# A MoE kernel with attention beside it: the late attention writes x transposed and normalises it by products with ones

## The chip, the core and the metric

The kernel runs on one NeuronCore of a Trainium2 chip. The metric is the device time of one execution in microseconds; the median of several runs is compared. The engines are TensorE (PE, with its weight loads PEld), VectorE (DVE), ScalarE (ACT), GpSimd (POOL) and SyncE (SP, whose queue issues most DMAs).

## The reference

Attention in chunks, then an RMS norm and a gated MoE layer on its output. Cut to what matters:

```
# attention: 4 batches, 8 heads, 768 positions, 64 per head; chunks of 32
scores = (q_chunk @ concat(mem_k, k[c-16 : c+32+8]).T) / 8          # 8 memory rows
a = exp(scores - max); a = a / (sum(a) + 1e-9)
out_chunk = a @ concat(mem_v, v[same rows])
x = out as (3072 tokens, 512)
xn = x / sqrt(mean(x*x) + 1e-6) * rms_g
g = xn @ w_gate; val = xn @ w_val                                   # 512 -> 1536
y = (g * sigmoid(g) * val) @ w_out                                  # 1536 -> 512
```

All data are float32.

## The kernel before

**Blocks and units.** The 3072 tokens are 8 blocks of 384. A block is half of one batch's sequence; its attention consists of 4 units, a unit being two heads of the half sequence. Units 0 to 7 (batch 0, blocks 0 and 1) are computed ahead of everything ("early"); units 8 to 31 are "late", in pairs, beside the MoE of the blocks before them.

**The MoE.** To keep float32 precision, each float32 operand is split into a high and a low part (type float32r), and a product is three passes: high by high, high by low, low by high. For one block, `f` runs over 12 slices of 128 of the hidden width. A round of `f` is: gate, 12 products into `pg` (`moe_in`, L591); value, 12 products into `pv` (L591); output of the slice before, 9 products into `po` (`moe_out`, L629). On the side, ACT makes the tanh of the gate (L598), DVE forms `t` (L602, L605), ACT casts `t` to its high part `hh` (L255 of the helper `copy`), DVE subtracts to get `hl` (L614). `t`, `hh` and `hl` have one buffer each.

**One late unit.** `load_qk` brings q and k by eight DMAs of SyncE's queue; `load_v` copies the memory rows on ACT and POOL and brings v. `stage_t` transposes q and k in 32x32 blocks on DVE (L315, L320) and copies the overlap of the chunks on ACT (L328, L329). `stage_s` (L346) makes the scores of 12 chunks on PE; `stage_m` takes the maximum and subtracts it on DVE (L358, L364); `stage_e` the exponential on ACT (L369). A step later `stage_p` transposes the weights on PE (L377), `stage_c` copies them out (L255, L258), `stage_o` multiplies with v on PE (L398): queries lie on partitions, and a 65th column of ones in v gives the sum of the weights. `stage_r` (L412, L416, L421, all DVE) divides and writes x, tokens on partitions.

**Norm and block end.** When the four units of a block are there, `stage_n` takes the squares with their sums on ACT (L428), the power -1/2 on GpSimd (L442), and scales x on DVE and ACT (L449, L451). At the end of the MoE block, `split_x` transposes x by 12 PE transposes (`stage_xt`, L470), and `stage_xh` (ACT, L475) and `stage_xl` (DVE, L480) make the high and low parts `xh`, `xl` for the next block, with the gain `rg`. The order on PE there: transposes of three tiles, the output round of f = 10, transposes of the last tile, the output round of f = 11.

**What sets the order.** Up to the 17th round the order on every engine is written out by hand in `ORDER` (one token per step; `tok_R` holds the first late unit's preparation). After it a list scheduler issues, on each engine, the instruction with the lowest position in the program that its own timing says is ready; `tc.high_priority()` lets a block pass what was written before it, `tc.issue_after(i)` puts instructions behind `i` on that engine, and PE's instructions are kept in program order (`on_pe`). The generator `late_steps` yields the attention's steps; `VISITS` says after which half round of a block (slot 2f after the gate of f, slot 2f+1 after its values) the next one is taken: "v" is the visit with transposes, scores and outputs of a pair, "t" the transposes of q and k of another unit, "n" the norm, "p" the last pair's transposes. There are seven such segments: the rest of block 0 from f = 5, then blocks 2 to 7; the first, the five in the middle and the last (no attention) differ.

**Buffers that matter.** PSUM: three rotating buffers (`psum_a`), and one each under the names "g", "v" (gate and value) and "o0" to "o2". SBUF: three staging buffers of 512 columns (`obuf`, tag "stg"), one x (tag "x"), one q and one k of a late unit ("qn", "kn").

Of the kernel before, what the change touches and what calls it, by code (L numbers as in the profile page):

```python
# [34 lines left out]
YMAX = 0x1DFE / 0x1000 * 2.0 ** -96  # L35


VISITS = (((1, "v"), (4, "t"), (5, "v"), (8, "t"), (11, "v"), (12, "n")),
# [31 lines left out]
def tile_kernel(ctx: ExitStack, tc: tile.TileContext, q, k, v, mem_k, mem_v,  # L70
# [71 lines left out]
    def late_pt():  # L142

        late["pt", 1] = p1.tile([P, NQ], F32, name="pt1", tag="wy")
        nc.vector.memset(late["pt", 1], 0.0)
        late_views("pt", 1)

    def late_views(n, i):
# [25 lines left out]
    def load_qk(u):  # L174
        b, hf, g = units[u]
        h0 = 2 * g
        t0 = hf * HT
        d = st.setdefault(u, {})
        if u < NE:

            k0 = t0 - hf * CH
            for n, src, r0, rows in (("q", q, t0, HT), ("k", k, k0, HT + CH)):
                x = d[n] = early.tile([P, 8, D], F32, name=f"{n}f{u}", tag=f"{n}f{u % NG}")[0:rows // 4]
                nc.sync.dma_start(out=x.rearrange("p (h r) d -> p h (r d)", h=2),
                                  in_=src[b, h0:h0 + 2, r0:r0 + rows].rearrange("h (p r) d -> p h (r d)", r=4))
            return

        d["q"] = qn = p1.tile([P, NC, CH], F32, name=f"qn{u}", tag="qn")
        d["k"] = kn = p1.tile([P, NC + 1, CH], F32, name=f"kn{u}", tag="kn")
        k0 = t0 - hf * CH  # L190
        for w in range(4):
            hh, e = w // 2, CH * (w % 2)
            nc.sync.dma_start(out=qn[CH * w:CH * w + CH],
                              in_=q[b, h0 + hh, t0:t0 + HT, e:e + CH].rearrange("(c p) d -> p c d", p=CH))
            nc.sync.dma_start(out=kn[CH * w:CH * w + CH],  # L195
                              in_=k[b, h0 + hh, k0:k0 + HT + CH, e:e + CH].rearrange("(c p) d -> p c d", p=CH))

    def load_v(u):
        stage_v(u)
        dma_v(u)  # L200

    def stage_v(u, e="a"):
# [5 lines left out]
        if hf == 0 and g == 0 and b > 0:  # L208
            for cp in range(2):
                nc.sync.dma_start(out=memV[64 * cp:64 * cp + NM], in_=mem_v[b].rearrange("h m d -> m h d"))  # L210
# [207 lines left out]
    def stage_rc(u, x):  # L418
        g = units[u][2]
        d = st.pop(u)  # L420
        nc.vector.tensor_tensor(out=x[:, :, 2 * g:2 * g + 2, :], in0=d["o3"][:, :, :, 0:D],  # L421
                                in1=d["r"].unsqueeze(3).broadcast_to([P, NT, 2, D]), op=ALU.mult)

    def squares(x, g0, g1, ss):

# [291 lines left out]

    late_x = {}

    def behind_last(u):  # L720
        done = next(i for i in reversed(nc.cur_bb.bb.instructions) if i.engine == nc.vector.engine)
        with tc.issue_after(done):
            stage_t(u)

    def late_steps():
# [3 lines left out]
        for n in range(len(pairs) + 1):  # L729
# [2 lines left out]
            new = pairs[n + 1] if n + 1 < len(pairs) else ()  # L732
            for u in old[0:1]:
                if u % NG == 0:
                    late_x["x"] = new_x()
            x = late_x.get("x")
            with tc.high_priority():
                for i, u in enumerate(old):
# [5 lines left out]
            with tc.high_priority():  # L744
                for u in cur:
                    stage_s(u)
                for u in cur:
                    stage_m(u)
                for u in cur:
                    stage_e(u)  # L750
                for i, u in enumerate(old):
                    stage_o(u, "v" if cur and i else None)
                for u in old:
                    stage_r(u, x)
                for u in new[0:1]:
                    behind_last(u)
            for u in new[0:1]:
                load_qk(u + 1)
            for u in cur if n else ():
                load_v(u)  # L760
            yield "v"
            if n and n % 2 == 0:
                with tc.high_priority():
                    stage_n(x)
                yield "n"
            if new:
                with tc.high_priority():
                    behind_last(new[1])
# [45 lines left out]

    def tok_N(n):
        sp["ss"] = stage_n0(blk["x"])
# [76 lines left out]
            for eng in (nc.vector.engine, nc.scalar.engine, nc.gpsimd.engine, nc.sync.engine)]  # L893
    manual.__exit__(None, None, None)

    behind = ExitStack()
    for i in ends:
        behind.enter_context(tc.issue_after(i))
    with tc.high_priority():
        late_buffers(0)  # L900
        stage_t(NE + 1)
    load_v(NE + 1)
    load_qk(NE + 2)
    pinned.append(True)

    def split_x(x, first, rest):

        xh = p1.tile([P, NKT, HT], F32R, name="xh", tag="xh")
        xl = p1.tile([P, NKT, HT], F32R, name="xl", tag="xl")
        with tc.high_priority():  # L910
            for kt in range(NKT):
                if kt == NKT - 1:
                    first()
                stage_x(xtiles(x), xh, xl, kt)
        rest()
        return xh, xl

    last1 = len(SEQ) - 1
    po1 = sp["po", 1]
    with tc.high_priority():  # L920
        prev = moe_hl(sp["t", last1], moe_hh(sp["t", last1]))
    xs = xs01[0]
    todo = late_steps()
    for sg, (blk, f0) in enumerate(segments):
# [7 lines left out]
        for f in range(f0, NF):  # L932
# [12 lines left out]
            if f < NF - 1:  # L945
                out_()
                prev = moe_h(g, vv)
            elif last:
                out_()
                finish(f, g, vv, po, blk)  # L950
            else:
                prev = moe_h(g, vv)
                xs = split_x(late_x["x"], out_, lambda: moe_out(NF - 1, prev, po))
        if sg == 0:
            behind.close()
        if not last:
# [29 lines left out]
```

## Time and profile before

| | us |
|---|---|
| three runs | 727.26, 727.30, 729.69 (median 727.3) |
| the profiled execution | 725.66, of which 723.9 span |
| PE busy | 708.6 (98%) |
| ACT busy | 284.2 (39%) |
| POOL busy | 35.5 (5%) |
| chain that ended last, share of PE | 89% |

How to read a page: each line of a group gives the kernel's line, engine, operation, written and read tiles, shapes and the count; after the bar the busy time, the mean of one in ns, and after the second bar the idle time of the engine ahead of it with its releasers. In the chain of waits each row is a start, a length and what ran or was waited for. Matmuls are pipelined: the row of one lasts longer than the distance to the next, so the time that one takes of the queue is read from start to start.

### The profile page before, as it was taken

Reading aid. Unit: us, or ns where it says so; the run is one execution under the profiler, and the core shown is the slowest. Engines: PE = TensorE matmul, PEld = TensorE weight load, DVE = VectorE, ACT = ScalarE, POOL = GpSimd, SP = SyncE. Lnnn points to the kernel's source line nnn. Section 1 sums busy time; section 2 is a strip of 40 time slices with the busy share of each in tenths; the row PEclk is TensorE's granted clock in tenths of the full one; section 3 lists DMA queues with packets and bytes.
Section 4 is the critical chain, followed back from the end, with each engine's and each line's share of the span. In section 5 each row is a group of like instructions: output and inputs, shape, how many; then the busy total and the mean of one; then the engine's idle time right before and its main releaser. Section 6 shows DMA issues by size and latency. Waiting matters only on the chain.

```text
span 723.9 us, 13126 instructions
## 1 busy us (share of the span) xinstructions
PE 708.6 (98%) x5136; PEld 656.0 (91%) x5136; DVE 382.1 (53%) x727; ACT 284.2 (39%) x600; POOL 35.5 (5%) x143
## 2 busy tenths in 40 slices
PE   7889999999999999999999999999999999999997
PEld 7778999998989999999999999999998999999997
DVE  3888999975663625444273534536254332432222
ACT  4899666543353315332153312433143221331112
POOL 3300000010010001000010000000010000000000
PEclk8999999999999999999999999999999999999999
DMA  8994554425532402304041120413111110010001
GB/s 173 206 255 147 175 194 127 125 46 123 97 60 75 78 9 42 77 11 84 0 77 52 34 53 1 84 44 66 18 35 28 44 39 1 1 45 0 1 1 43
DMA packets 143173, 50.20 MB, mean 69 GB/s; under 512 B 126984, under 2 KB 134536, under 8 KB 143112
## 3 DMA queue, kind: packets, MB, share of 16 engines
q1 hardware_dynamic: 139832, 44.49, 26.8%
q10 hardware_dynamic: 3280, 4.88, 1.9%
q8 instruction: 40, 0.66, 0.4%
q14 instruction: 21, 0.17, 0.1%
HBM read 43.06 MB, written 6.29 MB: 68 GB/s over the span
## 4 chain that ended last, share of the span: by engine, by line
PE 89%; ACT 4%; DVE 2%; DMA 2%; issue 1%; SPq 1%; POOL 0%; ACTq 0%; DVEq 0%; POOLq 0%
PE po L629 27%; PE pv L591 26%; PE pg L591 26%; PE s L346 3%; PE o L398 2%; PE xT L470 1%; PE pT L377 1%; ACT junk L428 1%; DMA memV<-in_mem_v_dram 1%; ACT pt L255 1%; DMA kv<-in_v_dram 1%; ACT qb L255 0%; ACT wy L539 0%; ACT ws L538 0%; SPq L195 0%
## 5 line engine op out<-in xcount | busy, mean ns | idle before, releaser
L591 PE MATMUL pg<-xh,wh_g 128*128 128x384 f32 x384 | 130.0, 339 | 0.7 <-DVE t L602 0.7
L591 PE MATMUL pv<-xh,wl_v 128*128 128x384 f32 x384 | 129.5, 337 | 0.5 <-DVE wl_v L562 0.5
L591 PE MATMUL pv<-xh,wh_v 128*128 128x384 f32 x384 | 129.7, 338 | 0.0
L591 PE MATMUL pv<-xl,wh_v 128*128 128x384 f32 x384 | 129.6, 337 | 0.0
L591 PE MATMUL pg<-xh,wl_g 128*128 128x384 f32 x384 | 129.5, 337 | 0.0
L591 PE MATMUL pg<-xl,wh_g 128*128 128x384 f32 x384 | 129.4, 337 | 0.0
L255 ACT CAST hh<-t 128x384 fp32r<-128x384 f32 x95 | 48.6, 512 | 201.9 <-PE po L629 177.8
L629 PE MATMUL po<-wh_o,hh 128*128 128x512 f32 x285 | 114.7, 402 | 0.3
L629 PE MATMUL po<-wh_o,hl 128*128 128x512 f32 x285 | 113.1, 397 | 0.0
L602 DVE SCALAR_TENSOR_TENSOR t<-t,pg 128x384 f32<-128x384 f32 x96 | 53.0, 552 | 112.8 <-ACT t L598 112.4
L629 PE MATMUL po<-wl_o,hh 128*128 128x512 f32 x285 | 112.3, 394 | 0.0
L614 DVE TENSOR_TENSOR hl<-t,hh 128x384 fp32r<-128x384 f32 x95 | 52.5, 553 | 104.7 <-ACT hh L255 99.9
L598 ACT ACTIVATE t<-pg 128x384 f32<-128x384 f32 x96 | 47.1, 491 | 122.8 <-PE pg L591 114.9
L605 DVE TENSOR_TENSOR t<-t,pv 128x384 f32<-128x384 f32 x95 | 52.5, 553 | 75.5 <-PE pv L591 74.9
L591 PEld LDWEIGHTS pg<-xh,wh_g 128*128 128x128 f32 x384 | 72.0, 188 | 4.6 <-DVE t L602 0.9
L591 PEld LDWEIGHTS pg<-xl,wh_g 128*128 128x128 f32 x384 | 72.1, 188 | 3.5
L591 PEld LDWEIGHTS pv<-xh,wl_v 128*128 128x128 f32 x384 | 72.0, 188 | 0.8 <-DVE wl_v L562 0.8
L591 PEld LDWEIGHTS pv<-xh,wh_v 128*128 128x128 f32 x384 | 72.1, 188 | 0.4
L591 PEld LDWEIGHTS pv<-xl,wh_v 128*128 128x128 f32 x384 | 72.1, 188 | 0.3
L591 PEld LDWEIGHTS pg<-xh,wl_g 128*128 128x128 f32 x384 | 72.0, 188 | 0.0
L629 PEld LDWEIGHTS po<-wh_o,hl 128*128 128x128 f32 x285 | 53.5, 188 | 14.4 <-DVE hl L614 2.0
L629 PEld LDWEIGHTS po<-wh_o,hh 128*128 128x128 f32 x285 | 53.5, 188 | 10.5 <-ACT hh L255 1.7
(124 smaller groups left out, 772.3 us busy)
## 6 DMA issues: line engine op xcount, KB each, us to landing
kn<-in_k_dram SPq DMA_DIRECT2D x96, 52.0 KB
qn<-in_q_dram SPq DMA_DIRECT2D x96, 48.0 KB
out_dram<-ob ACTq DMA_DIRECT2D x18, 256.0 KB
ws<-in_moe_w_gate_dram SPq DMA_DIRECT2D x4, 1024.0 KB
ws<-in_moe_w_val_dram SPq DMA_DIRECT2D x4, 1024.0 KB
ws<-in_moe_w_out_dram SPq DMA_DIRECT2D x4, 1024.0 KB
kv<-in_v_dram SPq DMA_DIRECT2D x48, 84.0 KB
kv<-in_v_dram SPq DMA_DIRECT2D x48, 70.0 KB
```

The costliest lines, as they stand in the source:

```text
L255: return nc.scalar.copy(out, in_)
L346: on_pe(nc.tensor.matmul(s[64 * par:64 * par + 64, o:o + KC], lhsT=qb[:, c].rearrange("p s q -> p (s q)"), rhs=kw[:, c], start=True, stop= ...
L377: on_pe(nc.tensor.transpose(out=t[:, i * P:(i + 1) * P], in_=pe[:, i * P:(i + 1) * P], identity=ident))
L398: on_pe(nc.tensor.matmul(o[64 * par:64 * par + 64, c0:c0 + D + 1], lhsT=pt[:, i, 2 * par + hh].rearrange("p c q -> p (c q)"), rhs=d["v"][: ...
L428: nc.scalar.activation(junk[:, 0:(g1 - g0) * P], x[:, i, 2 * g0:2 * g1].rearrange("p h d -> p (h d)"), AF.Square, accum_out=ss[:, i:i + 1])
L470: on_pe(nc.tensor.transpose(out=t[:, i * P:(i + 1) * P], in_=tiles[i][:, kt * P:(kt + 1) * P], identity=ident))
L591: on_pe(nc.tensor.matmul(ps[:, 0:HT], lhsT=weight(a, n, f, kt), rhs=xs[c][:, kt], start=cnt == 0, stop=cnt == 3 * NKT - 1))
L598: nc.scalar.activation(t, g, AF.Tanh, scale=0.5)
L602: nc.vector.scalar_tensor_tensor(out=t, in0=t, scalar=1.0, in1=g, op0=ALU.add, op1=ALU.mult)
L605: nc.vector.tensor_tensor(out=t, in0=t, in1=vv, op=ALU.mult)
L614: nc.vector.tensor_tensor(out=hl, in0=t, in1=hh.bitcast(F32), op=ALU.subtract)
L629: on_pe(nc.tensor.matmul(po[i], lhsT=h[a][:, i * P:(i + 1) * P], rhs=weight(c, "o", f), start=f == 0 and n == 0, stop=f == NF - 1 and n == 2))
```

## The change

- A late unit's weights are normalised before they are transposed: `late_d` sets the two places outside the sequence to zero, sums the rows, adds 1e-9, takes the reciprocal and multiplies, all on DVE. It replaces `stage_r`.
- `late_o` swaps the operands of the output product: v is the stationary operand, the weights move, so that the result has head and dimension on partitions and tokens along the row. x is then a tile `xT` of 128 by 4 by 384, and no PE transposes at the block end are needed.
- `late_r` copies a unit's result into x on ACT, squares it on ACT into a staging buffer, and DVE adds up the squares of the four units.
- `late_n` splits the sum into two float32r parts, multiplies both by a matrix of ones on PE (which sums over the partitions and spreads the sum to all of them), and takes the inverse square root on ACT and DVE by a bit estimate and a polynomial; then DVE scales x with `rg` and it. It is cut into three "n" steps.
- `split_x` no longer transposes: it casts and subtracts x from SBUF. The last h of a block is made in two staging buffers instead of `hh`, `hl`.
- q and k of units 9 and 10 and the memory rows of batch 1 are loaded earlier, within the hand-written order; unit 10 in the buffer of x. The step's other loads move accordingly.
- `VISITS` has the new slots. In the diff below, the lines after `late_n` belong to the visit of step n in `late_steps` (`old` is the pair to finish, `cur` the pair to begin, `new` the next one), then to `tok_R` (n = 0 and n = 4), then to `split_x`.

```
-VISITS = (((1, "v"), (4, "t"), (5, "v"), (8, "t"), (11, "v"), (12, "n")),
-          ((2, "t"), (5, "v"), (8, "t"), (17, "v"), (18, "n"), (20, "t")),
-          ((5, "v"), (8, "t"), (17, "v"), (18, "n"), (20, "t")),
-          ((5, "v"), (8, "t"), (17, "p"), (18, "v"), (19, "n")))
+VISITS = (((1, "v"), (2, "t"), (5, "v"), (8, "t"), (9, "v"), (10, "n"), (11, "n"), (12, "n")),
+          ((0, "t"), (3, "t"), (5, "v"), (8, "t"), (17, "v"), (19, "n"), (20, "n"), (21, "n")),
+          ((1, "t"), (5, "v"), (8, "t"), (17, "v"), (19, "n"), (20, "n"), (21, "n")),
+          ((1, "t"), (5, "v"), (8, "t"), (17, "p"), (18, "v"), (20, "n"), (21, "n"), (22, "n")))
+RSQRT = (-0.49999831, 0.37499999, -0.31395044, 0.27418771)
...
+    one = const.tile([P, 1], F32R, name="one")
...
+        if u == NE + 2:
+            t = p1.tile([P, NT * DM], F32, name=f"qkn{u}", tag="x")
...
+    def late_d(u):
+        pe = st[u]["p"]
+        if units[u][1]:
+            nc.vector.memset(pe[64:P, NJ - 1, KC - RC:KC], 0.0)
+        else:
+            nc.vector.memset(pe[0:64, 0, NM:NM + LC], 0.0)
+        r = p2.tile([P, NJ], F32, name=f"r{u}", tag="r")
+        nc.vector.tensor_reduce(out=r, in_=pe, axis=AX.X, op=ALU.add)
+        nc.vector.tensor_scalar(out=r, in0=r, scalar1=1e-9, scalar2=None, op0=ALU.add)
+        nc.vector.reciprocal(out=r, in_=r)
+        nc.vector.tensor_tensor(out=pe, in0=pe, in1=r.unsqueeze(2).broadcast_to([P, NJ, KC]), op=ALU.mult)
+
+    def late_o(u, tag=None):
+        pt, vw = pt_of(u), st[u]["v"]
+        o = psum_m(tag, f"o{u}") if tag else psum_a(f"o{u}")
+        for j in range(NJ):
+            for hh in range(2):
+                on_pe(nc.tensor.matmul(o[64 * hh:64 * hh + 64, j * D:(j + 1) * D], lhsT=vw[:, j, hh, 0:D],
+                                 rhs=pt[:, j // 2, 2 * (j % 2) + hh].rearrange("p c q -> p (c q)"),
+                                 start=True, stop=True))
+        st[u]["o"] = o
+
+    def late_r(u, x):
+        g = units[u][2]
+        o = st.pop(u)["o"]
+        nc.scalar.copy(x[:, g], o[:, 0:HT])
+        s = obuf(f"sq{u}")[:, 0:HT]
+        nc.scalar.activation(s, x[:, g], AF.Square)
+        if g:
+            nc.vector.tensor_tensor(out=s, in0=s, in1=late["ss"], op=ALU.add)
+        late["ss"] = s
+
+    def late_n(x):
+        ss = late["ss"]
+        sh, sl = [p3.tile([P, DM], F32R, name=f"s{c}", tag="stg")[:, 0:HT] for c in "hl"]
+        nc.scalar.copy(sh, ss)
+        nc.vector.tensor_tensor(out=sl, in0=ss, in1=sh.bitcast(F32), op=ALU.subtract)
+        yield
+        ps = psum_a("ssum")[:, 0:HT]
+        for i, c in enumerate((sh, sl)):
+            on_pe(nc.tensor.matmul(ps, lhsT=one.broadcast_to([P, P]), rhs=c, start=not i, stop=i == 1))
+        s = obuf("rs")[:, 0:HT]
+        nc.vector.tensor_scalar(out=s, in0=ps, scalar1=DM * 1e-6, scalar2=None, op0=ALU.add)
+        r = obuf("rr")[:, 0:HT]
+        nc.scalar.activation(r.bitcast(I32), s.bitcast(U32), AF.Copy, bias=float(0x5F3759DF), scale=-0.5)
+        t = obuf("rt")[:, 0:HT]
+        nc.vector.tensor_tensor(out=t, in0=r, in1=r, op=ALU.mult)
+        nc.vector.tensor_tensor(out=t, in0=t, in1=s, op=ALU.mult)
+        nc.vector.tensor_scalar(out=t, in0=t, scalar1=1.0, scalar2=None, op0=ALU.subtract)
+        yield
+        q = obuf("rq")[:, 0:HT]
+        nc.vector.tensor_scalar(out=q, in0=t, scalar1=RSQRT[3], scalar2=RSQRT[2], op0=ALU.mult, op1=ALU.add)
+        nc.vector.tensor_tensor(out=q, in0=q, in1=t, op=ALU.mult)
+        for c in (RSQRT[1], RSQRT[0]):
+            nc.vector.scalar_tensor_tensor(out=q, in0=q, scalar=c, in1=t, op0=ALU.add, op1=ALU.mult)
+        nc.vector.scalar_tensor_tensor(out=r, in0=q, scalar=1.0, in1=r, op0=ALU.add, op1=ALU.mult)
+        yield
+        for kt in range(NKT):
+            nc.vector.scalar_tensor_tensor(out=x[:, kt], in0=x[:, kt], scalar=rg[:, kt:kt + 1], in1=r,
+                                           op0=ALU.mult, op1=ALU.mult)
+        yield
...
+                for u in new[0:1] if n == 1 else ():
+                    behind_last(u)
                 for u in cur:
                     stage_e(u)
                 for i, u in enumerate(old):
-                    stage_o(u, "v" if cur and i else None)
+                    late_o(u, "v" if cur and i else None)
                 for u in old:
-                    stage_r(u, x)
-                for u in new[0:1]:
+                    late_r(u, x)
+            norm = late_n(x) if n and n % 2 == 0 else ()
+            if norm:
+                with tc.high_priority():
+                    next(norm)
+            if n == 1:
+                load_qk(new[0] + 1)
+            with tc.high_priority():
+                for i, u in enumerate(cur):
+                    if norm and i:
+                        with tc.issue_after(last_of(nc.vector)):
+                            late_d(u)
+                    else:
+                        late_d(u)
+                for u in new[0:1] if n not in (1, 2) else ():
                     behind_last(u)
...
+            load_mem(1)
...
+            load_qk(NE + 1)
             load_v(NE)
-            load_qk(NE + 1)
+            load_qk(NE + 2)
...
+    def split_x(x, t, first, rest):
...
+        first()
         with tc.high_priority():
+            with ExitStack() as behind:
+                behind.enter_context(tc.issue_after(last_of(nc.vector)))
+                for kt in range(NKT):
+                    nc.scalar.copy(xh[:, kt], x[:, kt])
+                    nc.vector.tensor_tensor(out=xl[:, kt], in0=x[:, kt], in1=xh[:, kt].bitcast(F32), op=ALU.subtract)
+                    if kt == 0:
+                        h = [p3.tile([P, DM], F32R, name=f"h{c}", tag="stg")[:, 0:HT] for c in "hl"]
+                        nc.scalar.copy(h[0], t)
+                        nc.vector.tensor_tensor(out=h[1], in0=t, in1=h[0].bitcast(F32), op=ALU.subtract)
+                        for eng in (nc.scalar, nc.vector):
+                            behind.enter_context(tc.issue_after(last_of(eng)))
+        rest(h)
```

More of the change, by code (lines that the diff above doesn't have):

```diff
@@ L146, in late_pt @@
         late_views("pt", 1)
+        nc.vector.tensor_copy(out=one, in_=ones[0][:, 1, 0:1])
     def late_views(n, i):
@@ L200, in load_v, with load_mem @@
         dma_v(u)
+    def load_mem(b):
+        for cp in range(2):
+            nc.sync.dma_start(out=memV[64 * cp:64 * cp + NM], in_=mem_v[b].rearrange("h m d -> m h d"))
     def stage_v(u, e="a"):
@@ L207, in stage_v @@
         d["v"] = vw = unit_tile(u, [P, NJ, 2, D + 1], "vw", NG)
-        if hf == 0 and g == 0 and b > 0:
-            for cp in range(2):
-                nc.sync.dma_start(out=memV[64 * cp:64 * cp + NM], in_=mem_v[b].rearrange("h m d -> m h d"))
+        if hf == 0 and g == 0 and b > 1:
+            load_mem(b)
         mv = memV[:, h0:h1].unsqueeze(1).broadcast_to([P, NJ, 2, D])
@@ L718, in tile_kernel, with last_of @@
     late_x = {}
+    def last_of(eng):
+        return next(i for i in reversed(nc.cur_bb.bb.instructions) if i.engine == eng.engine)
     def behind_last(u):
-        done = next(i for i in reversed(nc.cur_bb.bb.instructions) if i.engine == nc.vector.engine)
-        with tc.issue_after(done):
+        with tc.issue_after(last_of(nc.vector)):
             stage_t(u)
@@ L751, in late_steps @@
                 for i, u in enumerate(old):
-                    stage_o(u, "v" if cur and i else None)
+                    late_o(u, "v" if cur and i else None)
                 for u in old:
-                    stage_r(u, x)
-                for u in new[0:1]:
+                    late_r(u, x)
[8 more added lines that the diff above has]
+                    if norm and i:
+                        with tc.issue_after(last_of(nc.vector)):
+                            late_d(u)
+                    else:
+                        late_d(u)
+                for u in new[0:1] if n not in (1, 2) else ():
                     behind_last(u)
-            for u in new[0:1]:
+            for u in new[0:1] if n > 2 else ():
                 load_qk(u + 1)
-            for u in cur if n else ():
-                load_v(u)
+            with tc.issue_after(last_of(nc.scalar)) if n > 2 else ExitStack():
+                for u in cur if n not in (0, 2) else ():
+                    load_v(u)
             yield "v"
-            if n and n % 2 == 0:
+            for _ in norm:
+                yield "n"
+            if n == 2:
                 with tc.high_priority():
-                    stage_n(x)
-                yield "n"
+                    behind_last(new[0])
+                load_qk(new[1])
+                for u in cur:
+                    load_v(u)
+                yield "t"
             if new:
@@ L899, in tile_kernel @@
     with tc.high_priority():
+        prev = moe_hl(sp["t", last1], moe_hh(sp["t", last1]))
+        for eng in (nc.vector, nc.scalar):
+            behind.enter_context(tc.issue_after(last_of(eng)))
         late_buffers(0)
@@ L902, in tile_kernel @@
     load_v(NE + 1)
-    load_qk(NE + 2)
+    load_qk(NE + 3)
     pinned.append(True)
-    def split_x(x, first, rest):
+    def split_x(x, t, first, rest):
         xh = p1.tile([P, NKT, HT], F32R, name="xh", tag="xh")
         xl = p1.tile([P, NKT, HT], F32R, name="xl", tag="xl")
+        first()
         with tc.high_priority():
[L911 to L915, printed above, removed]
+            with ExitStack() as behind:
[8 more added lines that the diff above has]
+                        for eng in (nc.scalar, nc.vector):
+                            behind.enter_context(tc.issue_after(last_of(eng)))
+        rest(h)
         return xh, xl
[L918 to L921, printed above, removed]
     xs = xs01[0]
@@ L951, in tile_kernel @@
             else:
[L952 to L953 removed]
+                with tc.high_priority():
+                    t = silu_a(g)
+                    silu_b(t, g)
+                    moe_m(t, vv)
+                xs = split_x(late_x["x"], t, out_, lambda h: moe_out(NF - 1, h, po))
         if sg == 0:
```

10 lines of the change are left out of this document (7 added, 3 removed).

## The prediction

> **What bounds the kernel now.** I read the page's busy table first, then a table of stretches, then the chain of waits inside one late visit, then TensorE's instructions in order of time at the end of a block.
>
> ```profile
> PE 708.6 (98%) x5136; PEld 656.0 (91%) x5136; DVE 382.1 (53%) x727; ACT 284.2 (39%) x600; POOL 35.5 (5%) x143
> ```
>
> ```profile
> 162.77:218.20 55.43, 53.51 (x484) 48.86 (x482) 34.94 (x73) 23.86 (x60) 4.68 (x21) 1.00 0.48 94
> 473.37:558.43 85.06, 85.01 (x613) 79.14 (x613) 39.29 (x80) 27.44 (x65) 2.85 (x11) 1.00 0.19 41
> 642.02:723.90 81.88, 78.08 (x405) 72.35 (x405) 21.82 (x43) 16.19 (x33) 0.00 (x0) 1.00 0.06 20
> ```
>
> Columns of the stretches: length, then busy time of PE, PEld, DVE, ACT and POOL, the granted clock, the DMA share. From 218 us on, a block with late attention beside it lasts 85.06 us, and PE is busy for 85.01 of them at the full granted clock of 1.00. So in the late stretch the time is the length of TensorE's own queue: what leaves that queue is gained in full, what enters it is lost in full, and the other engines (39 and 27 us of 85) count only where PE has to wait for them. The stretch 162.77 to 218.20 is the rest of block 0, where the first late units arrive; 55.43 less 53.51, that is 1.92 us, is idle there. The early attention ahead of the MoE and the last block (from 642.02), which has no attention beside it, are hardly touched by the change.
>
> One late visit, by the chain of waits (start, length, what):
>
> ```profile
> 530.05 2.12 PE pv L591 x12
> 532.17 0.66 PE pT L377 x6
> 532.83 1.60 PE s L346 x48
> 534.42 1.40 PE o L398 x35
> 535.83 2.30 PE po L629 x9
> 538.13 2.12 PE pg L591 x12
> 540.25 2.12 PE pv L591 x12
> 542.36 2.08 PE po L629 x9
> ```
>
> The MoE runs in rounds: 12 gate products in 2.12 us, 12 value products in 2.12, 9 output products in 2.08. A visit puts three pieces of attention between them, 0.66 + 1.60 + 1.40 = 3.66 us, two visits per block.
>
> The end of the same block, TensorE alone:
>
> ```profile
> 554.83 1.14 PE L470 MATMUL xT<-ident,x 128*128 128x128 f32 x9
> 555.73 0.48 PE L629 MATMUL po<-wh_o,hh 128*128 128x512 f32 x1
> ...
> 557.89 0.49 PE L470 MATMUL xT<-ident,x 128*128 128x128 f32 x3
> 558.43 0.50 PE L629 MATMUL po<-wh_o,hh 128*128 128x512 f32 x1
> ...
> 560.74 0.34 PE L591 MATMUL pg<-xh,wh_g 128*128 128x384 f32 x1
> ```
>
> From the first transpose of x (554.83) to the next block's first gate product (560.74) are 5.91 us. In them lie 12 transposes of x and two output rounds of 9.
>
> **The change, part by part.** *Block end.* With x made transposed, the 12 transposes at the block end go, and TensorE only has two output rounds, 2 x 2.08 = 4.16 us. The difference, 5.91 - 4.16 = 1.75 us, holds the transposes (555.73 - 554.83 = 0.90, and 0.54 from 557.89 to 558.43) and a remainder of 0.31 in the last round, where `hh` and `hl` come late: now they must wait for the output round before, which still reads the single buffer of each. The change puts this last pair in the staging buffers, so it can be made during that round. What must be on time in its place: `xh`, `xl` of the first tile and the pair, one after the other on ACT and DVE. From the rows of the next fence that is about 0.55 (last product of t) + 0.51 (cast) + 0.55 (subtract) + 0.51 + 0.55 = 2.7 us after the value products, and the second half is wanted at 2.08 + 2 x 0.23 = 2.5 us if both tiles' work goes in strict turn; the four steps overlap between the two engines (the cast of the pair beside the subtraction of the tile), which brings 2.2. I take no wait, and keep 0.3 per block end for the range. Six block ends (the rest of block 0 and five full ones): 6 x 1.75 = 10.5 us gained.
>
> *Products with ones.* Two matmuls of 128x128 by 384 columns per block, the shape of a gate product: 2.12/12 = 0.177 each, 0.35 per block, 6 x 0.35 = 2.1 us lost. They stand between rounds of the same kind, so I add no change-over; if they wait for their operands it is more (below).
>
> *Attention products.* The output products swap operands: 12 per unit as before, 64 columns instead of 65. In the rows 48 products of s (64 columns) take 1.60 and 48 of o take 1.40, so the width does not show; 1/65 of 1.40 over 12 visits is 0.26 us at best. I count zero. The extra row sums that were column 65 move to DVE.
>
> *Other engines.* Prices per instruction, from the groups by shape (count | busy us, mean ns):
>
> ```profile
> L358 DVE TENSOR_REDUCE mx<-s 128x6 f32<-128x384 f32 x32 | 17.7, 552 | 7.5 <-PE s L346 7.2
> L412 DVE TENSOR_SCALAR r<-o 128x6 f32<-128x6 f32 x32 | 4.9, 154 | 0.5 <-PE o L398 0.5
> L416 DVE RECIPROCAL r<-r 128x6 f32<-128x6 f32 x32 | 6.0, 190 | 0.9
> L421 DVE TENSOR_TENSOR x<-o,r 128x384 f32<-128x384 f32 x32 | 17.7, 556 | 0.9
> L602 DVE SCALAR_TENSOR_TENSOR t<-t,pg 128x384 f32<-128x384 f32 x96 | 53.0, 552 | 112.8 <-ACT t L598 112.4
> L255 ACT CAST hh<-t 128x384 fp32r<-128x384 f32 x95 | 48.6, 512 | 201.9 <-PE po L629 177.8 <-DVE t L605 22.2 <-DVE ws L548 1.8
> L679 DVE MEMSET mhalf<- 128x3 f32 x1 | 0.1, 61 | 0.0
> ```
>
> late_d per unit: a small memset 0.06, reduce 0.55, add 0.15, reciprocal 0.19, product 0.56, together 1.5 us, where the old stage_r had 0.15 + 0.19 + 0.56 = 0.9. The sums of squares add three additions of 0.55 per block, the split of the sum one. The norm is a chain of 12 DVE instructions of 384 columns (one addition, three for t, five for the polynomial, counting the last into r, three further scalings after the first) and one more scaling: 13 x 0.55 = 7.2 us, and 0.5 on ACT; the power on GpSimd and the scaling of x go. DVE's 39.3 us per block thus become about 39.3 + 4 x 0.6 + 4 x 0.55 + 7.2 - 1.0 = 50 of 83: no bound by its sum. ACT gets four copies of o and four squares, each of 384 columns like the cast at 0.51, and loses six squares with their reads and the scaling: about even. All of it lies beside the MoE rounds, if the order on DVE allows. That is the question of the visits:
>
> ```profile
> 536.23 0.15 DVE L412 TENSOR_SCALAR r<-o 128x6 f32<-128x6 f32 x1
> ...
> 537.53 0.56 DVE L421 TENSOR_TENSOR x<-o,r 128x384 f32<-128x384 f32 x1
> 538.01 1.17 DVE L315 STREAM_TRANSPOSE qb<-qn 64x384 f32<-64x384 f32 x2
> 539.21 0.61 DVE L320 STREAM_TRANSPOSE kv<-kn 128x416 f32<-128x416 f32 x1
> 539.74 0.52 DVE L614 TENSOR_TENSOR hl<-t,hh 128x384 fp32r<-128x384 f32 x1
> ```
>
> ```profile
> 539.06 0.50 ACT L255 CAST hh<-t 128x384 fp32r<-128x384 f32 x1
> ```
>
> Here `hl`, which the output round at 542.36 wants for its third product (at about 542.83), stands in DVE's queue behind the high-priority work of the visit and ends at 540.26: 2.57 us in hand. In the visit that ends a block, late_d for two units in place of the r chain (537.53 + 0.56 - 536.23 = 1.86) adds 3.0 - 1.86 = 1.1, two additions of squares 1.1, the split 0.55: 2.8 us if all of it stands ahead of `hl`, so 0.2 us late; in the other visit 1.1 + 0.55 = 1.7, in time. The scheduler fills DVE with what is ready, and the second late_d is made to queue behind the split, which itself waits for ACT's squares, so `hl` may well slip in front. I take 0.15 us for each of the five visits that end a block with new units behind them, 0.75 in all; the ends are 0 and, with the first new unit's transposes (1.17 + 0.61) ahead of `hl` as well, 0.9 for each of 11 visits (9.9), where half of the 1.8 is made up by the time in hand.
>
> *Loads ahead.* The idle time of block 0's rest:
>
> ```profile
> PE pT L377 <- DVE t L602: 1.4, 1, 1.4
> ```
>
> ```profile
> 176.90 1.95 DMA qn<-in_q_dram
> ...
> 178.87 0.58 DVE qp L315
> ...
> 180.24 0.45 DVE t L602
> 180.74 0.87 PE pT L377 x6
> ```
>
> PE waits 1.4 us for the MoE step L602, which is held on DVE behind the transposes L315, and those wait in DVE's queue for q of a late unit to land at 178.85. The transposes of that step now find q and k of three units loaded in advance, one of them in its own buffer, and one step less waits for a landing. I take the 1.4 us as gained; ends 0 (the wait moves to the next unit's load, which shares the queue with v) and 1.92 (all idle of the stretch). The loads themselves move ahead in SyncE's queue, past the v loads of unit 8; nothing on PE waits for those until the first late visits.
>
> Moving the transposes of the second new unit into the next block's slot 1 leaves 4 slots before their use; the three norm slots keep PE's order free of a product whose operands are not ready: the split ends some 8.5 us into the visit's 3.66 + 3 x 2.1 = 10 us.
>
> *Sum.* -10.5 + 2.1 + 0.75 - 1.4 = -9.05 us. The profiled execution took 725.66 us (723.9 span, 1.8 around it), so it would take 716.6; the median of the three runs shown is 727.3, 1.6 above, and by the same difference I forecast 718.3.
>
> **The rivals.** *DVE late in the visits.* The work added to DVE pushes `hl`, or L602 that frees the gate's PSUM buffer, behind the point where PE wants it. For it: only 2.57 us in hand against up to 2.8 added, and then the transposes' 1.8 us too where they follow late_d. Against: half of the added work waits for ACT, and `hl` is ready before it. At 0.3 us (a late `hl` alone) to 0.9 us (`hl` and then L602 behind it) in 11 visits it costs 3.3 to 9.9 in place of 0.75: 720.8 to 727.4. [...]
>
> *The loads ahead bring nothing.* Then 719.7: the wait at 180 comes back in another visit, as the third visit is now two slots earlier (slot 9 after slot 8), with 13's transposes just before it.
>
> *Slower: x comes late at the block end.* Now x is ready 10 us before the transposes need it; after the change the chain ones product, 7.2 us on DVE, 0.5 on ACT, first xh and xl (1.1) stands between the norm slot and the next block's gate. PE's cover is 8 rounds (16.8 us) in four blocks and 6 rounds (12.6 us) in the first and the last. With the MoE's own DVE work in that stretch (4 x 0.55 = 2.2) the chain is about 11 us. It decides when it takes over 12.6: each us beyond is lost at six ends. To be slower by over 0.5% (3.6 us) than 727.3 it must eat 12.7 us, 2.1 at each end, 732 or so; that needs chains of 15 to 19 us, so handovers of a whole round each.
>
> **How the numbers follow.** Forecast, 716 to 720.5: 0.54. DVE late: 0.25, six tenths of it under 723.7. Loads bring nothing, the rest as forecast: 0.12. Slower: 0.04. Better than forecast (under 716; no cost in the visits, o narrower, all idle gone): 0.05. A measurement can tell about 0.5%, 3.6 us, from no change: faster 0.54 + 0.15 + 0.12 + 0.05 = 0.86, within 0.10, slower 0.04. Range: from 715.0 (727.3 with 10.5, 1.92 and 0.26 gained, 2.1 lost and no cost in the visits is 716.7, less the 1.6 between profiled and median run) to 723.7 (the nearer six tenths of the DVE rival).
>
> **What would show it.** Right: a steady block of 83.5 to 83.9 us instead of 85.06; between the last value products and the next gate 4.2 us; no xT group on PE; a group of 12 ones products at about 340 ns; no wait of pT for L602 near 180. Wrong: PE idle before po with `hl` or L602 as releaser (DVE rival), before pg with xl as releaser at block ends (slower), or DVE transposes in the first late block still waiting for q or k.

## The result and the profile after

The changed kernel takes 716.81 us (median of 5 runs, 715.69 to 717.03) against 727.35 us for the kernel before: a ratio of 0.984, 95% interval 0.982 to 0.986. The forecast was 718.3. The profiled execution took 716.4 us, 714.6 of it span.

The busy table of the page after, then stretches of the same kernel (length, busy time of PE, PEld, DVE, ACT, POOL, granted clock, DMA share):

```profile
PE 697.6 (98%) x5076; PEld 648.1 (91%) x5076; DVE 434.1 (61%) x860; ACT 288.4 (40%) x582; POOL 31.7 (4%) x137
```

```profile
162.50:219.55 57.05, 54.72 (x482) 49.48 (x482) 46.11 (x105) 25.10 (x57) 3.56 (x18) 1.00 0.40 83
386.22:469.55 83.33, 83.33 (x603) 78.13 (x602) 47.89 (x102) 28.19 (x62) 2.31 (x12) 1.00 0.23 47
552.89:635.32 82.43, 82.29 (x555) 76.43 (x554) 38.20 (x77) 24.58 (x52) 0.30 (x1) 1.00 0.07 19
635.32:714.60 79.28, 75.42 (x397) 70.42 (x395) 20.70 (x41) 14.86 (x31) 0.00 (x0) 1.00 0.06 21
```

A steady block went from 85.06 to 83.33 us, and PE is still busy throughout. DVE rose from 39 to 48 us of it (50 had been worked out), without a wait of PE. But the rest of block 0 has 57.05 - 54.72 = 2.3 us of idle PE, not less than before. These stretches begin with a block's first gate product, those shown before with its last output round. From first gate product on, the last block took 79.56 us before and takes 79.28 now, and the block ahead of it went from 83.60 to 82.43.

The end of a block, TensorE alone, and the same stretch in the chain of waits:

```profile
465.45 0.40 PE L707 MATMUL po<-wh_o,hh 128*128 128x512 f32 x1
...
469.55 0.33 PE L669 MATMUL pg<-xh,wh_g 128*128 128x384 f32 x1
```

```profile
465.61 4.10 PE po L707 x18
469.71 2.10 PE pg L669 x12
```

Two output rounds follow each other without a gap: 469.55 - 465.45 = 4.10 us, where 5.91 stood. So it is at the four middle block ends. At the first and the last end the two rounds take 4.67 and 4.68 us, where 6.14 and 5.92 stood. The last one, DVE, ACT and the start of PE's last round:

```profile
629.73 2.20 DVE L498 SCALAR_TENSOR_TENSOR xT<-xT,rg,rr 128x384 f32<-128x384 f32 x4
631.85 0.55 DVE L683 TENSOR_TENSOR t<-t,pv 128x384 f32<-128x384 f32 x1
632.43 0.52 ACT L1027 CAST hh<-t 128x384 fp32r<-128x384 f32 x1 [1.07 <-DVE t L683]
633.00 0.50 PE L707 MATMUL po<-wh_o,hh 128*128 128x512 f32 x1
```

The norm's last slot lies behind the gate of the block's last f there, one later than at a middle end. Its four scalings of x stand on DVE ahead of L683, the block's last product, which starts 1.2 us after PE's output round (630.64) where it starts 0.2 us after it at a middle end (465.65 against 465.45). The last h is late by that, and the two rounds lose 0.57 and 0.58 us.

The visit that ends a block, in the chain of waits:

```profile
442.53 0.66 PE pT L388 x6
443.19 1.60 PE s L357 x48
444.79 1.40 PE o L454 x48
446.19 2.28 PE po L707 x9
448.47 2.12 PE pg L669 x12
450.58 2.11 PE pv L669 x12
452.70 0.35 PE ssum L479 x2
453.05 2.08 PE po L707 x9
```

The three attention pieces take 0.66, 1.60 and 1.40 us as before (the outputs 1.40 with 64 columns as with 65), and the two ones products add 0.35.

What PE waited for in the rest of block 0, and DVE's instructions ahead of the first of these waits (the bracket is the idle time before, with its releaser):

```profile
PE pT L388 <- DVE t L680: 1.4, 1, 1.4
...
PE ssum L479 <- DVE sl L475: 0.5, 1, 0.5
...
PE ssum L479 <- ACT sh L474: 0.3, 1, 0.3
```

```profile
170.19 0.55 DVE L443 TENSOR_REDUCE r<-kv 128x6 f32<-128x384 f32 x1
172.51 0.57 DVE L326 STREAM_TRANSPOSE qp<-qn 64x384 f32<-64x384 f32 x1 [1.76 <-DMA qn<-in_q_dram]
...
176.49 0.52 DVE L446 TENSOR_TENSOR pe<-pe,r 128x384 f32<-128x384 f32 x1
176.93 1.15 DVE L326 STREAM_TRANSPOSE qb<-qkn 64x384 f32<-64x384 f32 x2
178.09 0.61 DVE L331 STREAM_TRANSPOSE kv<-qkn 128x416 f32<-128x416 f32 x1
178.62 0.52 DVE L692 TENSOR_TENSOR hl<-t,hh 128x384 fp32r<-128x384 f32 x1
179.75 0.55 DVE L680 SCALAR_TENSOR_TENSOR t<-t,pg 128x384 f32<-128x384 f32 x1 [0.62 <-ACT t L676]
```

The wait of pT for the MoE's first step is there as before, 1.4 us. The cause has moved: the unit loaded ahead (10, `qkn`, its last DMA issued at 165.59) is at hand, but unit 11's transposes (`qp<-qn`) were put ahead of it on DVE, in the middle of late_d, and DVE stood 1.76 us until their q landed. Unit 10's were tied behind the end of late_d, which came behind that. And the ones products of the first late block, one slot after their visit, wait 0.3 + 0.5 us for their operands; in later blocks, two slots after, they don't.

**Theory.** The gain is the block end (transposes and the late last pair: 1.81 us at each of the four middle ends, 1.47 and 1.24 at the first and the last, 9.95 in all), less 0.35 per block for the ones products; loads and visits give nothing. **Rivals:** the loads or the new order of the visits carry part of it; the last pair is on time only because the transposes went; and, since the sum of the terms falls short, something makes the MoE products themselves faster. Averaged from start to start in the steady blocks, a gate product took 175.4 ns before and 174.8 after.

### The profile page after: what moved, and what is told of

It reads as the page before. It is cut to its first block, busy times and chain, and to the rows that moved or that the text cites. A ratio compares the mean times of both kernels' runs of the same rounds, so it can differ in the third digit from the quotient of the medians.

```text
span 714.6 us, 13091 instructions
## 1 busy us (share of the span) xinstructions
PE 697.6 (98%) x5076; PEld 648.1 (91%) x5076; DVE 434.1 (61%) x860; ACT 288.4 (40%) x582; POOL 31.7 (4%) x137
## 4 chain that ended last, share of the span: by engine, by line
PE 88%; DVE 4%; ACT 4%; DMA 2%; issue 1%; SPq 0%; POOL 0%; ACTq 0%; POOLq 0%; DVEq 0%
PE po L707 27%; PE pg L669 27%; PE pv L669 27%; PE s L357 3%; PE o L454 2%; PE pT L388 1%; DMA ws<-in_moe_w_val_dram 1%; DMA memV<-in_mem_v_dram 1%; ACT pt L266 1%; ACT junk L506 0%; ACT ws L616 0%; DVE xT L498 0%; ACT qb L266 0%; DVE kw L269 0%; DVE mx L369 0%
## 5 line engine op out<-in xcount | busy, mean ns | idle before, releaser
L266 ACT CAST hh<-t 128x384 fp32r<-128x384 f32 x89 | 45.5, 511 | 178.9 <-PE po L707 149.5
L680 DVE SCALAR_TENSOR_TENSOR t<-t,pg 128x384 f32<-128x384 f32 x96 | 52.5, 547 | 87.7 <-ACT t L676 87.4
L692 DVE TENSOR_TENSOR hl<-t,hh 128x384 fp32r<-128x384 f32 x89 | 49.4, 555 | 84.1 <-ACT hh L266 83.9
L683 DVE TENSOR_TENSOR t<-t,pv 128x384 f32<-128x384 f32 x95 | 52.5, 552 | 59.7 <-PE pv L669 58.9
```

What stands on the lines that cost most here:

```text
L266: return nc.scalar.copy(out, in_)
L680: nc.vector.scalar_tensor_tensor(out=t, in0=t, scalar=1.0, in1=g, op0=ALU.add, op1=ALU.mult)
L683: nc.vector.tensor_tensor(out=t, in0=t, in1=vv, op=ALU.mult)
L692: nc.vector.tensor_tensor(out=hl, in0=t, in1=hh.bitcast(F32), op=ALU.subtract)
```

## The experiments

Times are medians; every ratio is to the kernel before, run on the same chip, with its 95% interval. The kernel before took 727.33 to 727.75 us beside these runs, so a difference between two of them can be off by 0.4 us. "A steady block" is one of the four from block 2 to block 5, from first gate product to first gate product.

**The changed kernel once more (e1).** No edit.

> The changed kernel as it is, once more. If the MoE products' pace (174.7 ns per gate or value product, against 175.4 in the kernel before) belongs to the program, it comes back within 0.2 ns and the time is 716 to 717.5 us; if it belongs to the single execution, the pace lies anywhere from 174.5 to 175.5 ns.

717.33 us, ratio 0.986 (0.984 to 0.987); a gate product takes 174.8 ns again and the steady block 83.33 us to the hundredth. The pace belongs to the program. What varies between executions is the beginning: the first gate product starts at 51.29 us in one and at 53.12 in the other, and the wait near 180 us was 1.42 and 0.52.

**The last h back in its single buffers (e2).**

```
-                        h = [p3.tile([P, DM], F32R, name=f"h{c}", tag="stg")[:, 0:HT] for c in "hl"]
+                        h = [p1.tile([P, HT], F32R, name=c, tag=c) for c in ("hh", "hl")]
```

> The changed kernel with the last h of a block back in the single buffers hh and hl. Theory (the waits of the last output round, 0.31 us at each of six block ends, went because of the staging buffers): 1.5 to 2.2 us longer than the changed kernel, 718.5 us, and the last output round waits for hh and hl again. Rival (they went because the transposes went): within 0.4 us.

721.7 us, ratio 0.992 (0.990 to 0.993), 4.4 above e1: the direction of the theory, twice its size. The steady block is 84.14, 0.81 more. The chain at its end:

```profile
469.79 1.84 PE po L707 x8
471.63 0.02 issue
471.65 0.52 ACT hh L1027
472.17 0.04 issue
472.22 2.47 PE po L707 x9
```

ACT starts `hh` at 471.65, 0.02 us after the eighth product of the output round before, the last one that reads the old `hh`. PE stands idle for 0.38 us of the 0.52 that this takes (84.14 us long, 83.76 busy), and the last round takes 2.47 instead of 2.1, since `hl` comes late as well. In the kernel before, three transposes (0.33 us, at 558.06 in its chain) stood at this place and covered part of that wait. The two parts of the change at the block end need each other.

**That part alone, in the kernel before (e5).** The last h in two staging buffers, the transposes kept.

```
-                prev = moe_h(g, vv)
+                prev = [p3.tile([P, DM], F32R, name=f"h{c}", tag="stg")[:, 0:HT] for c in "hl"]
```

> The kernel before with one part of the change alone: the last h of a block in two staging buffers. Theory (both waits of the last output round come from the single buffers): 1.5 to 2.2 us shorter than the kernel before, 725.4 us, the wait behind hh and hl gone from the block ends. Rival (ACT and DVE are held by xh and xl of the transposed x there, so that h comes no earlier): within 0.5 us of before.

726.28 us, ratio 0.998 (0.996 to 0.999). The block end takes 5.48 us instead of 5.91, the steady block 84.79, 0.27 less than before, and the last round no longer waits:

```profile
557.16 2.08 PE po L629 x9
559.24 0.33 PE xT L470 x3
559.57 2.09 PE po L629 x9
```

2.09 stands where 2.47 stood. So the buffers alone take out the wait, 0.43 us at an end, as the theory has it. The size in time is 1.2 us by the medians and 1.7 by the ratio (0.6 to 2.8 by its interval), too coarse to tell it from the 1.5 to 2.2 expected. The gate products were slightly slower in this kernel (175.75 ns against 175.38), which hides part; the last section comes back to that.

**The transposes put back (e6).** 12 PE transposes at the block end of the changed kernel, results unused.

```
+        for kt in range(NKT):
+            pj = psum_a(f"xT{kt}")
+            for i in range(NT):
+                on_pe(nc.tensor.transpose(out=pj[:, i * P:(i + 1) * P], in_=x[:, kt, i * P:(i + 1) * P], identity=ident))
+            if kt == NKT - 2:
+                first()
```

> The changed kernel with 12 PE transposes of x put back at each block end, in the places that they had; their results are not used. Theory (the transposes' own length on TensorE, 0.90 + 0.54 less the waits in it, was what the change gained): 8 to 9.5 us longer than the changed kernel, 725.5 us, and 0.7 us more where x of the first late block is not yet scaled. Rival (the gain came from other steps on ACT and DVE): under 4 us longer.

724.54 us, ratio 0.996 (0.995 to 0.998), 7.2 above e1: most of the gain is gone.

```profile
305.79:390.46 84.67, 84.67 (x615) 79.34 (x614) 47.86 (x101) 28.13 (x62) 2.30 (x12) 1.00 0.22 46
```

1.34 us more per steady block (84.67 against 83.33), and 1.39 at its end (5.49 us against 4.10). With the 0.43 us of e5 that makes up the 1.81. The whole is less than the 8 to 9.5 us expected: the 1.44 of the prediction still held part of the wait for `hh`, and the block ahead of the last grew by 0.99 only (83.42 against 82.43); my estimate is that the transposes cover part of the 0.58 us that the last end loses to its late h. The rival falls.

**Ones products twice (e8).** The loop over the two products runs two times; the norm's scale changes with it.

> The changed kernel with the ones products made twice (four instead of two per block; the sum, and so the norm's scale, is doubled). Theory (each pair costs its length on TensorE and nothing else): 6 x 0.35 = 2.1 us longer, 718.9 us. Rival (their result is waited for, so the second pair delays the chain to the block end as well): more than 3 us.

718.77 us, ratio 0.988 (0.987 to 0.990).

```profile
304.63:388.32 83.69, 83.69 (x605) 78.47 (x604) 47.94 (x102) 28.22 (x62) 2.30 (x12) 1.00 0.22 47
```

0.36 us more in a steady block, the length of two products. Nothing waits for the later result, at the first and the last block end no more than elsewhere (4.67 us both), so the rival by which the ones products delay x stays out.

**Loads not ahead (e7).** Units 9 and 10 and the memory rows load where they did before, unit 11's transposes in slot 4.

> The changed kernel with the loads of units 9 and 10 and of the memory rows back where they were, and the transposes of unit 11 in slot 4. Theory (the loads ahead gained nothing): within 0.6 us of the changed kernel, the wait near 179 us between 1.0 and 1.9 us. Rival (they bought the slots 9 to 12 of the first block): 1.5 us longer or more, with waits in the visits at slots 5 or 9.

718.31 us, ratio 0.988 (0.986 to 0.989), 1.0 above e1, between the two expectations. The wait is one of another instruction:

```profile
PE s L357 <- DVE qp L269: 1.6, 1, 1.6
```

From the last hand-ordered double round to the second block's first gate product, PE's queue takes 72.66 us here, 72.05 and 71.17 in the two profiles of the changed kernel. That is 0.6 to 1.5 us more, so "nothing" was too little. But e7 has unit 11's transposes in slot 4 as well, so its partner is e4 below, which differs from it in the loads alone: 70.40 us. Between these two the loads ahead are worth 2.3 us of the stretch (1.1 by the medians, 1.7 by the ratios). Part of what they could give was not collected.

**Unit 11 in its turn (e3, e4).** e3 ties unit 11's transposes behind unit 10's; e4 moves them to slot 4.

```
-        with tc.issue_after(last_of(nc.vector)):
+        with tc.issue_after(last_of(nc.vector)), tc.issue_after(kept.get(u - 1) or last_of(nc.vector)):
             stage_t(u)
+        if u == NE + 2:
+            kept[u] = last_of(nc.vector)
```

```
-VISITS = (((1, "v"), (2, "t"), (5, "v"),
+VISITS = (((1, "v"), (4, "t"), (5, "v"),
```

> The changed kernel with one more order on VectorE: unit 11's transposes behind unit 10's, whose q and k are there. Theory (the wait of 1.42 us at 179 us stands because unit 11's transposes were put ahead and hold VectorE until their q lands at 172.5 us): the wait goes or falls under 0.4 us, 1.0 to 1.5 us shorter, 715.5 us. Rival (VectorE is short of time there whatever the order): the wait stays over 1 us.

> The changed kernel with the transposes of unit 11 two slots later (slot 4 of block 0's rest, where they were before). Theory: they then stand behind unit 10's without an order of their own, the wait at 179 us falls under 0.4 us, 715.5 us. Rival: unit 12's loads, which go out behind them, come later and the third visit waits instead: no gain, 716 to 717.5 us.

In both the wait for L680 is gone; of PE's waits in the late part only those of the ones products are left. The same stretch:

```profile
147.57:218.11 70.54, 69.64 (x561) 63.48 (x561) 58.73 (x127) 31.89 (x70) 8.13 (x39) 1.00 0.38 76
```

70.54 us in e3 and 70.40 in e4 against 72.05 and 71.17: 0.6 to 1.7 us better, and PE's idle time in it falls from 2.33 (changed kernel: 72.05 long, 69.72 busy) to 0.90. In time, 716.82 and 717.18 us, ratios 0.985 (0.984 to 0.987) and 0.986 (0.984 to 0.988), it can't be told from e1: the beginning varies by more (first gate product at 51.29 and 53.12 us).

**More work on DVE (e11).** Three more instructions of 0.55 us in each late_d.

```
+        for _ in range(3):
+            nc.vector.tensor_tensor(out=pe, in0=pe, in1=pe, op=ALU.max)
```

> The changed kernel with three more VectorE instructions of 0.55 us per late unit at the end of late_d (a maximum of the weights with themselves, which changes nothing), 3.3 us more per visit. The tightest rows of the changed kernel are the gate's buffer, freed 1.2 to 1.5 us before it is wanted in the visits that end a block, and 1.9 us in the others. Theory (the visits have that much in hand and no more): TensorE waits 0.5 to 2 us in a visit, 8 to 20 us in all, 725 to 737 us. Rival (the scheduler finds other places, VectorE is 61% busy): under 3 us longer.

722.27 us, ratio 0.993 (0.991 to 0.994), 4.9 above e1. Neither expectation holds as it stands, but the place tells:

```profile
150.10:226.28 76.18, 71.39 (x561) 64.73 (x561) 65.32 (x142) 32.04 (x69) 8.15 (x39) 0.98 0.35 70
310.02:393.45 83.43, 83.43 (x604) 78.04 (x602) 53.10 (x114) 28.27 (x62) 2.31 (x12) 1.00 0.23 47
```

A steady block grew by 0.10 us with 5.2 us more of busy DVE. Four to five of the 4.9 us are in the rest of block 0 (76.18 against 72.05 and 71.17), where the visits follow each other in 4 slots. PE stands idle there for 4.8 us instead of 2.3; the other 1.7 us of the 4.1 (76.18 less 72.05) are longer busy time, in a stretch whose granted clock was 0.98 instead of 1.00 in this execution. So 3.3 us more per visit cost next to nothing in the steady blocks: the scheduler places `hl` and the MoE's first step on `t` (L680) between the instructions of late_d (in the visit at 367 us `hl` starts at 373.40, between two of the added ones), and my theory of "that much in hand and no more" is wrong there.

**The place of the operands (e9, e10).** What is left is the pace. The changed kernel has one constant more, `one`, of 4 bytes; the built program gives it 32 bytes in each partition (it lies at byte 81184, the next constant at 81216), and x, t, the staging buffers and the weights of f = 10 and 11 lie 32 bytes further on. e9 gives the kernel before such a tile (the first diff), e10 takes the shift out of the changed kernel (the second).

```
+    pad = const.tile([P, 1], F32, name="pad")
     mhalf = const.tile([P, NT], F32, name="mhalf")
```

```
-    one = const.tile([P, 1], F32R, name="one")
-    mhalf = const.tile([P, NT], F32, name="mhalf")
+    both = const.tile([P, NT + 1], F32, name="mhalf")
+    mhalf, one = both[:, 0:NT], both[:, NT:NT + 1].bitcast(F32R)
```

> The kernel before with nothing but a tile of 4 bytes more among the constants, so that x, t, the staging buffers and the last weights lie 32 bytes further on, as they do in the changed kernel. Theory (the pace of the gate and value products, 175.5 ns in the kernel before and 174.81 in the changed one and its variants, goes with where the operands lie): 174.8 ns, and the five steady blocks 1.2 us shorter together than 423.8, the whole 1.5 to 2 us shorter than before. Rival (the pace goes with what ACT and VectorE do beside them): 175.4 to 175.7 ns, no change in time.

> The changed kernel with its constant of ones put in the same tile as another, so that everything lies where it lay in the kernel before. Theory of the place: 175.4 ns per gate or value product, 1.5 to 2 us longer than the changed kernel, 718.7 us. Rival: 174.8 ns, no change.

e9: 725.21 us, ratio 0.997 (0.996 to 0.998). The kernel before gets faster by an unused tile. e10: 720.4 us, ratio 0.989 (0.987 to 0.991), 3 us above e1. Both differences are a little larger than the 1.5 to 2 us expected. The chain of waits for the round of f = 7 (the start, the length, what), before and e9:

```profile
434.48 2.08 PE po L629 x9
436.56 2.12 PE pg L591 x12
438.68 2.12 PE pv L591 x12
```

```profile
433.83 2.04 PE po L630 x9
435.87 2.10 PE pg L592 x12
437.98 2.11 PE pv L592 x12
```

and e10, with the changed kernel's work at the old place:

```profile
430.31 2.08 PE po L707 x9
432.39 2.12 PE pg L669 x12
434.51 2.12 PE pv L669 x12
```

The steady block is 84.74 in e9 (85.06 before) and 83.61 in e10 (83.33): 0.3 us per block either way, with the same work. The mean gate product is 174.78 ns in e9 and 175.41 in e10, the values of the changed kernel and of the one before. The rival, ACT's and DVE's work beside, falls as the cause of this difference: e9 has the old work and the new pace.

**The late weights too (e12).** In the changed kernel the rounds of f = 0 to 4 were faster (11 intervals of a gate round take 1.906 to 1.920 us) than those of f = 5 to 11 (1.930 to 1.936). e12 moves the late weights, t and the staging buffers 32 bytes down, x stays; unit 11's transposes are in slot 4.

```
+    right = ctx.enter_context(tc.tile_pool(name="right", bufs=1, side="right")).tile([P, 8], F32, name="right")
     early_cm = tc.tile_pool(name="early", bufs=1, side="right")
...
-    mhalf = const.tile([P, NT], F32, name="mhalf")
+    both = const.tile([P, 2 * NT], F32, name="mhalf")
+    mhalf, sr1 = both[:, 0:NT], both[:, NT:]
...
-        sr = p1.tile([P, NT], F32, name="sr", tag="sr")
+        sr = sr1
```

> The changed kernel with the weights of f = 5 to 11, t and the staging buffers 32 bytes further down than it has them (x stays where it is) and unit 11's transposes in slot 4. Guess (a product is at its fast pace when x and the weights lie an odd number of 32-byte steps apart, as for f = 0 to 4 of the changed kernel, where 11 intervals take 1.906 us, and at the slow one of 1.930 us otherwise, as for f = 5 to 11): 1.906 us for all f, 0.35 us less per block, and with the wait at 179 us gone 713 to 715 us. Rival (only the place of x matters, or the pace goes with something else about these weights): 1.930 us stays for f = 5 to 11, 715.5 to 717 us.

713.7 us, ratio 0.981 (0.980 to 0.983): faster than both kernels. Unit 11's slot has its part in that (0.8 to 1.7 us in the stretch of e4); the place shows in the rows.

```profile
427.85 2.08 PE po L709 x9
429.93 2.08 PE pg L671 x12
432.01 2.08 PE pv L671 x12
```

f = 7 now takes 2.08 us per gate round, and 11 intervals take 1.906 to 1.913 us for every f from 5 on, as guessed. But the gate rounds of f = 2 to 4, which the guess has as fast, went from 1.910 to 1.916 up to 1.921 to 1.930, and some output rounds lost too (2.04 to 2.08), so the steady block fell by 0.25, not 0.35, to 83.08.

## Why the prediction was right, step by step

*The bound.* Right: in the steady blocks only the length of PE's queue counted, before and after (PE busy for 85.01 of 85.06 us and 83.33 of 83.33).

*Block end, -10.5 us.* Right in its mechanism; in size two misses cancelled in part. At the four middle ends the stretch went from 5.91 to 4.10 us (forecast 4.16). The prediction put 1.44 of its 1.75 us on the transposes and 0.31 on the wait; e6 and e5 make it 1.39 and 0.43, and e2 shows that without the staging buffers the wait would have grown. "I take no wait" failed at the first and the last end, where the norm's scalings of x stand ahead of the last product on DVE and cost nearly 0.6 us each. All six ends give 4 x 1.81 + 1.47 + 1.24 = 9.95 us: 0.2 more than forecast by the middle ones, 0.8 less by the two others.

*Ones products, +2.1 us.* Right in length (0.35, e8 0.36). That they wait for nothing failed once: 0.8 us in the first late block, where their slot follows the visit's directly. I had worked out that spacing for the steady blocks alone.

*Attention products, 0.* Right. (The row of o that was read for it counts 35 of the 48 records; the visit of the changed kernel counts all 48 in the same 1.40 us.)

*DVE in the visits, +0.75 us.* It cost nothing in the steady blocks, and e11 shows how much cover there is: three more instructions per late unit made a steady block only 0.10 us longer. The step that failed is that the added work stands ahead of `hl`: `hl` is ready first, and the list scheduler puts it there (in the visit shown it starts at 449.51, in the middle of the second late_d, 3 us ahead of the output round that reads it). In the stretch where it shows, DVE took its instructions in the order laid down: it stood 1.76 us until unit 11's q landed, and late_d's addition (L444), whose operand was done at 170.74, started behind that transpose, at 173.03. What the rival missed is that this order is laid down with the readiness in view. What DVE did cost came at the first and the last block end, as said above. (The time in hand of 2.57 us was read from a row of the chain; PE's own rows start that round at 542.20, so it was 2.4.)

*Loads ahead, -1.4 us.* Wrong in the profiled execution: the wait stayed at 1.42 us (0.52 in e1). The step that failed is "one step less waits for a landing": the transposes of unit 11, which does wait, went ahead of unit 10's. The prediction had named this as a sign against it (transposes of the first late block still waiting for q). e3 and e4 collect what was forecast, 0.6 to 1.7 us, and e7 against e4, 2.3 us, shows that the loads were needed for it.

*Not in the sum.* The products became faster by a shift of 32 bytes: 2.4 us by e9's ratio (0.0033 of 727.35; 1.6 to 3.1 by its interval), 0.3 us in every steady block. The prediction took the length of a MoE round as fixed, and its sign of a steady block of 83.5 to 83.9 us was missed for that, at 83.33.

*The sum.* The profiled execution took 716.4 us where 9.05 off 725.66 make 716.6, but that is luck in part. Up to block 2's first gate product the changed kernel gained 1.0 us, 0.2 of it ahead of the MoE, where the sum has 2.65 (1.75 and 1.4, less 0.35 and 0.15). The four steady blocks gained 1.7 each, where the sum has 1.25. The pace and the 0.75 that was not lost stand in for the 1.4 us, the 0.8 of the ones products and the 1.1 of the two late ends that did not come. The medians lie 1.5 us below the forecast of 718.3 since it carried over the 1.6 us by which the median of the kernel before lay above its profiled execution; for the changed kernel that is 0.4.

By pieces, a steady block fell by 1.73 us: 1.81 at its end, 0.35 back for the ones products, the rest pace (e10 against the changed kernel: 0.28). The three overlap by a hundredth or two.

## What to carry to other kernels

In the steady blocks, where PE's queue set the time (85.01 of 85.06 us busy), a step was worth its length in that queue: 1.39 us at a block end for the 12 transposes (e6), 0.36 us for two more products (e8). Price such a step from start to start, and check that what it covered has another cover, as the late pair of h did (without it, in e2, a steady block took 0.81 us more). The loads brought ahead were worth 2.3 us of their stretch with unit 11's transposes in slot 4 (e4 against e7); with those transposes ahead of unit 10's, waiting for their landing, 0.6 to 1.7 us of it was not collected: look at the order on the consumer's engine for such a neighbour. And a tile of 4 bytes moved x, t, the staging buffers and the last weights by 32 bytes, which changed the kernel before by 2.4 us (e9): measure the kernel before with the same shift before the gain is put down to the work.

## What the hardware showed that was not expected

The same products, in the same order, with the same neighbours, ran at 2.08, 2.10 or 2.12 us per 12 (128x128 by 384 columns) in kernels that differ in a shift of 32 bytes in a partition. With x at its old place (the kernel before and e10) the output, gate and value rows at f = 7 take 2.08, 2.12 and 2.12 us; with x 32 bytes further on (e9 and the changed kernel) they take 2.04, 2.10 and 2.11. Moving the late weights by 32 bytes took 11 intervals of a gate round from 1.930 or more to 1.913 or less for f = 5 to 11.

The place is not all of it. e5 leaves x and the weights where the kernel before has them, and yet 11 intervals of f = 0 to 2 take 1.922 to 1.943 us in four of its blocks, against 1.904 to 1.924. And within the kernel before, f = 3 takes 1.904 us and f = 4 takes 1.920 to 1.921 in blocks 2 to 6, but 1.921 and 1.904 in the last block, which has no attention beside it. So the place alone does not account for the pace; what else moves it, no run here tells. What the pace follows in the addresses stays open too: with x at its old place, rounds at 1.904 and 1.924 us stand side by side among weights of f = 0 to 4, and some output rounds went the other way in e12 (2.04 to 2.08). Only two places of x were tried.
